# Two 33-partition copies and two stores in place of four one-row copies and one store, at the end of a decode layer

## The chip, the cores and the metric

The kernel runs on one core of a Trainium2 chip. The metric is the device time of one execution in microseconds, as the median of several runs; the span in the profile (first to last instruction) is 1.25 to 1.4 us shorter than the time of the same run. Before the change the time was 202.92 us (three runs, 202.83 to 203.02).

## The reference

One token goes through an attention block over cached keys and values (32 heads of 128, 4096 positions), then through a gated feed-forward block, both with a layer norm ahead and a residual added:

```python
h  = x + attention(layernorm(x), k_cache, v_cache, wq) @ wo     # x is [1, 1, 640], bf16
g, u = layernorm(h) @ w_gate, layernorm(h) @ w_up               # 640 -> 1728
h2 = h + (gelu(g) * u) @ w_down                                 # 1728 -> 640: the result
```

The result is 640 numbers, 1280 B.

## The kernel before

The kernel keeps lists of operations per engine. `V`, `A`, `T` add one to VectorE, ScalarE and TensorE, with the operations that it depends on; `P.dma` adds a DMA issued by the named engine. Dependencies on another engine become waits on its semaphore, a counter that the other engine raises when it is done. In these traces an issue carries one such wait itself, and one that needs two has a wait instruction ahead of it: in that of before the store's issue waits for VectorE's semaphore, and a wait instruction of 17 ns ahead of it for ScalarE's.

The last product accumulates in PSUM (`psum` in the traces, which have it as the output of these matmuls), in one tile, `ps_d`, as four rows of 160 columns in partitions 0, 32, 64 and 96. From there it is copied to `out_row` in SBUF, from which the store reads it. The residual `h` is put into the same rows first:

```python
    out_row = sb("out_row", [1, D], BF16)
    ...
    def resid(e):
        for q in range(4):
            i = e.matmul(ps_d[32 * q:32 * q + 1, 0:160], ones_f[:, 0:1],
                         hX[:, 32 * q:32 * q + 32, :].rearrange("p a c -> p (a c)"), start=True, stop=False)
        return i
    ...
    def down(ms, qs=range(4)):
        def fn(e):
            for m in ms:
                for q in qs:
                    rows, wd = (128, wd_sb[:, m]) if m < 13 else (48, wd_lo[:, m - 13])
                    i = e.matmul(ps_d[32 * q:32 * q + 1, 0:160], hm[0:rows, m:m + 1],
                                 wd[0:rows, 160 * q:160 * q + 160], start=False, stop=(m == 12))
            return i
        return fn
    ...
    T(down(range(8, 12)), d_wd[2])
    dn = {q: T(down([12], [q]), d_wd[3]) for q in (0, 2, 1, 3)}
    os = [V(lambda e, q=q: e.tensor_copy(out_row[0:1, 160 * q:160 * q + 160], ps_d[32 * q:32 * q + 1, 0:160]), dn[q])
          for q in range(2)]
    os += [A(lambda e, q=q: e.copy(out_row[0:1, 160 * q:160 * q + 160], ps_d[32 * q:32 * q + 1, 0:160]), dn[q])
           for q in range(2, 4)]
    d_out = P.dma("sync", out[0, :, :], out_row[:, :], *os)
    P.op("sync", None, d_out)          # SyncE waits for the store to land: the end of the program
```

The softmax here doesn't subtract the row's maximum and nothing guards it: scores larger than these inputs give would overflow.

## Time and profile before

| | before |
|---|---|
| time, median | 202.92 us |
| span of the profiled run | 201.52 us |
| DMA engines | busy to nine tenths or more until the last fortieth of the span |
| landing of the last piece of w_down (160 KB) to the end | 2.41 us |
| landing of the piece before it (640 KB) to the end | 2.79 us |

The change concerns what comes after the last weights. The prediction below shows the lines of the page, the chain and the timeline for it.

For comparisons I use a **tail**: the time from the start of the last four matmuls of w_down to the end of the span. It leaves out the stream of loads, whose scatter is larger than the change (the four start at 199.17 and 199.39 us in the two traces of the changed kernel below). In the timeline of before, cut to a moment at which only those four run:

```profile
199.27 0.35 PE L525 MATMUL psum<-k_slot,hm 128*1 128x160 bf16 x4
```

The four start at 199.27 us, so the tail of before is 201.52 - 199.27 = 2.26 us (2.258 from the trace's records, which are in ns).

### The profile page before, as it was taken

Reading aid. Unit: us, or ns where it says so; the run is one execution under the profiler, and the core shown is the slowest. Engines: PE = TensorE matmul, PEld = TensorE weight load, DVE = VectorE, ACT = ScalarE, POOL = GpSimd, SP = SyncE. Lnnn points to the kernel's source line nnn. Section 1 sums busy time; section 2 is a strip of 40 time slices with the busy share of each in tenths; the row PEclk is TensorE's granted clock in tenths of the full one; section 3 lists DMA queues with packets and bytes.
Section 4 is the critical chain, followed back from the end, with each engine's and each line's share of the span. In section 5 each row is a group of like instructions: output and inputs, shape, how many; then the busy total and the mean of one; then the engine's idle time right before and its main releaser. Section 6 shows DMA issues by size and latency. Waiting matters only on the chain.

```text
span 201.5 us, 2014 instructions
## 1 busy us (share of the span) xinstructions
PE 122.1 (61%) x1008; PEld 34.7 (17%) x756; DVE 100.9 (50%) x51; ACT 12.6 (6%) x33; POOL 34.4 (17%) x36
## 2 busy tenths in 40 slices
PE   0108019759908953692469439907780789479685
PEld 0101000002200120102010201100120022169583
DVE  0200196885199169608950796199229901420321
ACT  2100000001000100010001001000100010010101
POOL 6400000000063008002600170053007200100000
PEclk9999999966985995899559957975998569855555
DMA  9999999999999999999999999999999999999992
GB/s 358 415 411 455 423 429 416 429 442 455 420 429 423 423 423 475 429 416 429 423 429 423 475 423 416 429 423 429 449 449 423 423 429 408 439 420 425 411 408 80
DMA packets 3849, 84.31 MB, mean 418 GB/s; under 512 B 450, under 2 KB 644, under 8 KB 1156
## 3 DMA queue, kind: packets, MB, share of 16 engines
q1 hardware_dynamic: 3842, 84.23, 97.7%
q8 instruction: 4, 0.07, 0.1%
q14 instruction: 1, 0.01, 0.0%
q10 hardware_dynamic: 2, 0.00, 0.0%
HBM read 84.23 MB, written 0.00 MB: 418 GB/s over the span
## 4 chain that ended last, share of the span: by engine, by line
DMA 68%; PE 19%; DVE 9%; SPq 3%; issue 1%; DVEq 0%
DMA v_slot<-in_A_v_cache_dram 42%; DMA k_slot<-in_B_w_down_dram 14%; DMA k_slot<-in_A_k_cache_dram 12%; PE psum L363 9%; PE psum L167 8%; DVE prod L375 6%; SPq L59 3%; DVE sc L381 2%; PE psum L352 1%; PE psum L525 0%; DVE out_row L534 0%; DVEq L114 0%
## 5 line engine op out<-in xcount | busy, mean ns | idle before, releaser
L375 DVE TENSOR_TENSOR prod<-k_slot,qb 128x8192 bf16<-128x8192 bf16 x16 | 75.2, 4737 | 6.8 <-DMA k_slot<-in_A_k_cache_dram 4.7
L167 PE MATMUL psum<-prod,id_b 128*128 128x512 bf16 x233 | 67.1, 445 | 0.0
L381 DVE TENSOR_REDUCE sc<-psum 128x128 f32<-128x2048 f32 x8 | 18.3, 2291 | 51.0 <-PE psum L167 51.0
L385 POOL TENSOR_TENSOR p_bd<-pt,own 128x512 bf16<-128x512 bf16 x6 | 28.3, 4715 | 85.3 <-ACT pt L382 85.3
L352 PE MATMUL psum<-prod,id_b 128*128 128x512 bf16 x23 | 10.6, 461 | 49.2 <-DVE prod L375 45.7
L363 PE MATMUL psum<-v_slot,p_bd 128*16 128x512 bf16 x224 | 17.8, 475 | 7.0 <-DMA v_slot<-in_A_v_cache_dram 7.0
L352 PEld LDWEIGHTS psum<-prod,id_b 128*128 128x128 bf16 x23 | 2.3, 99 | 70.3 <-DVE prod L375 47.6
L369 PEld LDWEIGHTS psum<-hs,po_sb 128*128 128x128 f32 x64 | 9.1, 208 | 23.9 <-issue 23.5
L363 PEld LDWEIGHTS psum<-v_slot,p_bd 128*16 128x16 bf16 x224 | 5.8, 105 | 39.7 <-DMA v_slot<-in_A_v_cache_dram 28.0
L392 ACT COPY po_sb<-psum 128x512 f32<-128x512 f32 x7 | 4.1, 586 | 73.6 <-PE psum L363 73.6
L369 PE MATMUL psum<-hs,po_sb 128*128 128x4 f32 x64 | 8.5, 256 | 0.1
L335 PE MATMUL psum<-arena,xlnB 128*32 128x512 bf16 x20 | 3.3, 626 | 7.2 <-DMA arena<-in_A_wq_dram 7.2
L382 ACT ACTIVATE pt<-sc,zero_t 128x128 bf16<-128x128 f32 x8 | 3.2, 401 | 71.1 <-DVE sc L381 71.1
L465 PE MATMUL psum<-aP,arena 128*128 128x1 bf16 x160 | 6.6, 178 | 0.0
L465 PEld LDWEIGHTS psum<-aP,arena 128*128 128x128 bf16 x160 | 6.5, 131 | 0.0
L389 POOL MEMSET spare<- 1x1 f32 x1 | 0.1, 89 | 36.4 <-DVE p_bd L385 36.4
L494 PE MATMUL psum<-hlnT,v_slot 128*128 128x1 bf16 x150 | 5.5, 173 | 0.8 <-issue 0.8
L340 DVE CAST qb<-psum 128x512 bf16<-128x512 f32 x1 | 0.7, 692 | 10.1 <-PE psum L167 10.1
L494 PEld LDWEIGHTS psum<-hlnT,v_slot 128*128 128x128 bf16 x150 | 5.3, 120 | 1.5 <-issue 0.9
L363 PE MATMUL psum<-k_slot,p_bd 128*16 128x512 bf16 x32 | 2.9, 520 | 2.8 <-DVE p_bd L385 2.8
L308 PE MATMUL psum<-one_bf,x_row 1*128 1x1 bf16 x5 | 0.4, 177 | 6.8 <-DMA x_row<-in_A_x_dram 6.8
L311 DVE COPY xx<-psum 128x5 f32<-128x5 f32 x1 | 0.2, 165 | 7.2 <-PE psum L308 7.2
(72 smaller groups left out, 34.8 us busy)
## 6 DMA issues: line engine op xcount, KB each, us to landing
k_slot<-in_A_k_cache_dram SPq DMA_DIRECT2D x8, 4096.0 KB, 25.9
v_slot<-in_A_v_cache_dram SPq DMA_DIRECT2D x7, 4096.0 KB, 17.2
arena<-in_A_wq_dram SPq DMA_DIRECT2D x1, 5120.0 KB, 15.2
arena<-in_A_wo_dram SPq DMA_DIRECT2D x2, 2560.0 KB, 35.2
k_slot<-in_A_v_cache_dram SPq DMA_DIRECT2D x1, 4096.0 KB, 26.8
v_slot<-in_B_w_gate_dram SPq DMA_DIRECT2D x1, 2160.0 KB, 23.7
k_slot<-in_B_w_down_dram SPq DMA_DIRECT2D x3, 640.0 KB, 29.2
v_slot<-in_B_w_up_dram SPq DMA_DIRECT2D x1, 1296.0 KB, 26.5
```

Source lines behind the costliest of these rows:

```text
L59: ev = self.op(eng, lambda e: e.dma_start(out, in_), *deps, dma=True, chan=chan)
L167: built = e.matmul(out, lhsT, rhs, start=start, stop=stop)
L335: mm = held if hf else lambda e, *a, **k: e.matmul(*a, **k)
L352: mm = held if n or not first else lambda e, *a, **k: e.matmul(*a, **k)
L363: i = e.matmul(ps_o[a:a + 16, :], p_bd[:, 4 * b:4 * b + 4, :].rearrange("p g j -> p (g j)"), vt[:, 4 * b:4 * b + 4, :], start=(b < 4), sto ...
L369: i = e.matmul(ps_a[:, bass.ds(at, 4)], po_sb[:, 128 * r:128 * r + 128], hs[:, r, :], start=(r == 0), stop=(r == 3))
L375: mults[G, i] = VM(lambda e: e.tensor_tensor(out=prod[:, i, :, :], in0=kt[:, 64 * i:64 * i + 64, :], in1=qb[:, G, :].unsqueeze(1).to_broad ...
L381: reds[G] = VR(lambda e: e.reduce_sum(sc[:, :], ps_f.rearrange("p (g d) -> p g d", d=16), axis=AX.X), folds[G, 1])
L385: blocks[G] = on(lambda e: e.tensor_tensor(out=p_bd[:, :, :], in0=pt[:, :].unsqueeze(2).to_broadcast([128, 128, 4]), in1=own[:, :].unsquee ...
L392: evs[G] = AS(lambda e: e.copy(po_sb[:, :], ps_o), pvs[G])
L465: r = e.matmul(ps_p[:, c:c + 1], wo_sb[:, i, c::5], aP[:, i:i + 1], start=False, stop=(i == 31), skip_group_check=True)
L494: i = e.matmul(ps[:, m:m + 1], ws, hlnT[:, c:c + 1], start=(c == 0 and m == 0), stop=(c == 4), skip_group_check=True)
```

## The change

The intent is to pay for one copy per engine instead of two. A copy of 33 partitions covers two of the four rows (partitions 0 and 32, or 64 and 96) and 31 rows of no interest. The result then lies in two SBUF rows, partitions 0 and 32, of 320 columns each. Each is stored by a DMA of its own, one issued by SyncE and one by ScalarE. So that a row holds adjacent columns of the result, the product's column blocks are dealt out in the order 0, 320, 160, 480.

```diff
-    out_row = sb("out_row", [1, D], BF16)
+    out_row = sb("out_row", [33, 320], BF16)
...
+    col = (0, 320, 160, 480)
     def resid(e):
         for q in range(4):
             i = e.matmul(ps_d[32 * q:32 * q + 1, 0:160], ones_f[:, 0:1],
-                         hX[:, 32 * q:32 * q + 32, :].rearrange("p a c -> p (a c)"), start=True, stop=False)
+                         hX[:, col[q] // 5:col[q] // 5 + 32, :].rearrange("p a c -> p (a c)"), start=True, stop=False)
...
-                                 wd[0:rows, 160 * q:160 * q + 160], start=False, stop=(m == 12))
+                                 wd[0:rows, col[q]:col[q] + 160], start=False, stop=(m == 12))
...
-    dn = {q: T(down([12], [q]), d_wd[3]) for q in (0, 2, 1, 3)}
-    os = [V(lambda e, q=q: e.tensor_copy(out_row[0:1, 160 * q:160 * q + 160], ps_d[32 * q:32 * q + 1, 0:160]), dn[q])
-          for q in range(2)]
-    os += [A(lambda e, q=q: e.copy(out_row[0:1, 160 * q:160 * q + 160], ps_d[32 * q:32 * q + 1, 0:160]), dn[q])
-           for q in range(2, 4)]
-    d_out = P.dma("sync", out[0, :, :], out_row[:, :], *os)
-    P.op("sync", None, d_out)
+    dn = [T(down([12], [q]), d_wd[3]) for q in range(4)]
+    os = [V(lambda e: e.tensor_copy(out_row[0:33, 0:160], ps_d[0:33, 0:160]), dn[1]),
+          A(lambda e: e.copy(out_row[0:33, 160:320], ps_d[64:97, 0:160]), dn[3])]
+    halves = out[0, :, :].rearrange("o (q n) -> (o q) n", q=2)
+    d_out = [P.dma(eng, halves[q:q + 1, :], out_row[32 * q:32 * q + 1, :], *os) for q, eng in enumerate(("sync", "scalar"))]
+    P.op("sync", None, *d_out)
```

## The prediction

Sum: -0.30 us for the copies, 0.20 for two issues at once, 0.02 at the end, -0.08 in all, so 202.84 us. The 0.20 is the estimate from the trace of before: the 225 ns by which ScalarE's issue at the head (497 ns) is longer than the lone issue of the store (272 ns). As its mark the prediction named a second issue of about 0.45 to 0.5 us. The prediction's lines from 1.28 us on are the issues at the head (start us, us). That the wait of one issue for another is what lengthens the issue at the head was not shown.

> **What bounds the kernel now.** I read the page of the profile first, then the chain of waits cut to the last 17 us, then the order of instructions in the last 3 us, then the durations of the instructions that touch the output row, and last the waits of SyncE. The page:
>
> ```profile
> span 201.5 us, 2014 instructions
> DMA  9999999999999999999999999999999999999992
> DMA 68%; PE 19%; DVE 9%; SPq 3%; issue 1%; DVEq 0%
> DMA v_slot<-in_A_v_cache_dram 42%; DMA k_slot<-in_B_w_down_dram 14%; DMA k_slot<-in_A_k_cache_dram 12%; PE psum L363 9%; PE psum L167 8%; DVE prod L375 6%; SPq L59 3%; DVE sc L381 2%; PE psum L352 1%; PE psum L525 0%; DVE out_row L534 0%; DVEq L114 0%
> ```
>
> The DMA engines are at nine tenths or more in 39 of 40 slices of 5.04 us: the kernel streams the caches and weights, and only the last slice is not bound by them. The chain gives the copies out of PSUM (DVE out_row) 0% of the span. The change touches nothing before the last weights but the order of residual columns, so all it can win lies in the last 2.8 us. The chain of waits there (start us, us, what):
>
> ```profile
> 198.74 0.04 issue
> 198.78 0.87 PE psum L525 x20
> 199.65 0.30 DVE out_row L534
> 199.95 0.03 issue
> 199.99 0.32 DVE out_row L534
> ```
>
> After the last piece of w_down has landed come 20 matmuls (0.87 us), then two VectorE copies in a row, 0.30 + 0.03 + 0.32 = 0.65 us. The timeline of the last microseconds (start us, us, engine, line, operation) has the same, with ScalarE beside it:
>
> ```profile
> 199.64 0.66 DVE L534 CAST out_row<-psum 1x160 bf16<-1x160 f32 x2 [2.64 <-PE psum L525]
> 199.68 0.60 ACT L536 CAST out_row<-psum 1x160 bf16<-1x160 f32 x2 [5.55 <-PE psum L525]
> 200.36 0.27 SPq L59 DMA_DIRECT2D out_dram<-out_row  x1
> ```
>
> ScalarE's pair ends at 200.28, VectorE's at 200.30, and SyncE begins to issue the store at 200.36, 0.06 us after the later. From there to the end of the span is 201.52 - 200.36 = 1.16 us (201.52 is the unrounded span), of which 0.27 us is the issue and the rest the store itself. Single durations (ns min/median/max), from the view of the output row, and SyncE's wait for the landing:
>
> ```profile
> L534 DVE CAST out_row<-psum x2: 311/314/316, 199.6 to 200.0; 1x160 bf16<-1x160 f32 x2
> L536 ACT CAST out_row<-psum x2: 285/286/287, 199.7 to 200.0; 1x160 bf16<-1x160 f32 x2
> SPq L114 <- DMA out_dram<-out_row: 0.9, 1, 0.9
> ```
>
> So the tail is a series: matmuls, copy, copy, issue, flight of the store.
>
> [...]the 128-partition casts of 512 columns took 692 ns (VectorE) and 586 ns (ScalarE), and a 128-partition copy of 5 columns 165 ns. A line through those two VectorE points has (692 - 165) / 507 = 1.04 ns a column and gives 165 + 155 x 1.04 = 326 ns for 160 columns of 128 partitions; one partition took 314. So 33 partitions should cost what one does.
> [...]
>
> ```profile
> 1.28 0.33 SPq L59 DMA_DIRECT2D k_slot<-in_A_k_cache_dram  x1
> 1.30 0.50 ACTq L59 DMA_DIRECT2D x_row<-in_A_x_dram  x1
> 1.66 0.71 SPq L59 DMA_DIRECT2D v_slot<-in_A_v_cache_dram  x1
> ```
>
> ScalarE's load of one 1280 B row, issued 0.03 us into a SyncE issue, took 497 ns; SyncE's own store of one 1280 B row, with nobody beside it, took 272. SyncE's next issue, begun while ScalarE's still ran, took 707 ns, where the same load later takes 327 to 328 ns.
> [...]No part of the trace before shows two stores at once.
> [...]
>
> **The change part by part.** Copies: two per engine become one of 33 partitions by 160 columns. On VectorE the gap between its two starts goes, 199.99 - 199.64 = 0.35 us, on ScalarE 199.99 - 199.68 = 0.31 us.
>
> Start of the copies: the four last matmuls start within 0.02 us of each other[...] (the 16 matmuls before take about 0.13 us a group of four: 20 in 0.87 us). Before, VectorE waited for the first of the four and ScalarE for the second; now VectorE waits for the second and ScalarE for the fourth. I charge 0.01 us to each: VectorE starts at 199.65, ScalarE at 199.69. With 0.314 and 0.286 us they end at 199.96 and 199.98. The later end was 200.30, so both rows are ready 0.32 us earlier. I take 0.30, as the ends of matmuls are modelled.
>
> The store: SyncE waits for the same two semaphores as before, so its issue starts at about 199.98 + 0.06 = 200.04. ScalarE's issue needs the end of its own copy and VectorE's, and starts at about the same time. Both are one row of 640 B instead of 1280. Halving the bytes is worth nothing much: the store occupies a DMA engine for part of one 0.03 us slice in a flight of 0.9 us[...].
>
> Two issues at once[...]. The head gives the size: ScalarE's issue was 497 - 272 = 225 ns longer than a lone one-row issue. [...]so I estimate 0.15 to 0.27 us and take 0.20 us for the second of the two. The last store then leaves 0.20 us after the first. SyncE waits for both, so it adds to the end in full.
>
> End: one more wait on SyncE. If ScalarE's store is last it has already passed the first wait; if its own is last, a satisfied wait follows, at most 0.06 us (from the step between VectorE's end and the issue above). I take 0.02.
>
> Sum: -0.30 + 0.20 + 0.02 = -0.08 us. The span goes from 201.52 to 201.44, the time from 202.92 to about 202.84.
>
> **The rivals.** *Rival A, the two issues do not wait for each other.* Then all of the 0.30 us stays and the time is 202.62. For it: [...]the head shows three issues in a crowd of other loads[...]. Against: the 497 ns, on a one-row transfer.
>
> *Rival B, the second queue costs more than it saves.* ScalarE's queue has lain idle since its one load at 1.3 us, its sequencer must see the end of its own copy before it can issue[...]. If ScalarE's issue takes the 0.50 us of the head, and starts 0.03 us late, the time is 202.92 - 0.30 + (0.50 - 0.27) + 0.03 + 0.02 = 202.90; if the flight also lengthens by 0.1 us, 203.00. For it: the 497 and 707 ns. Against: the tail has no other DMA in flight, since the traffic ended with w_down at 198.74.
>
> *Rival C, the copies get slower with 33 partitions.* [...]Against: the 128-partition rows above.
>
> *Rival D, a change upstream.* The residual matmuls only read other columns of the same tile, same shapes and count; all loads, their order and their waits stay. I expect nothing here but the scatter of the run times (202.83 to 203.02, 0.19 us), which is more than twice the change I predict.
>
> **Range and chances.** The mechanisms span 202.62 to 203.00. With 0.1 us of scatter to either side, 202.55 to 203.10 should hold it 8 times in 10. Two per cent is 4.06 us; the whole tail from the last landing to the end is 2.8 us and half of it is untouched, so faster by 2% is impossible by this route, and slower would need something that no view shows. I give within 2% a chance of 0.99.
>
> **What would show it right or wrong.** One VectorE and one ScalarE copy of 33x160, at 0.31 and 0.29 us, starting at 199.65 and 199.69 relative to the same landing of w_down; a slower copy makes rival C right. The two issues starting within 0.1 us of each other near 200.04: [...]two at about 0.27 show rival A. From the end of the later issue to the end of the span I expect 201.52 - 200.63 = 0.89 us as before; more is the longer flight of rival B. A different time of the last w_down landing would be scatter, and the tail must then be compared from that landing on. The prediction is wrong in its main step if the tail shortens by 0.25 us or more, or grows.

## The result and the profile after

| | before | after |
|---|---|---|
| time, median of the same rounds | 202.88 us (4 runs, 202.72 to 203.02) | 202.62 us (4 runs, 202.50 to 202.70) |
| span of the profiled run | 201.52 us | 201.24 us |
| tail in the profiled run | 2.258 us | 2.072 us |

The ratio is 0.9987, with a 95% interval from 0.9970 to 1.0004: by the times alone not even certain to be faster. A ratio here is the mean time of one kernel's fast runs over that of the other's of the same rounds, so it is not quite the ratio of the medians.

The tail tells more. The timeline of after, first at a moment when only the last four matmuls run, then from the copies on (start us, us, engine, line, operation):

```profile
199.17 0.34 PE L526 MATMUL psum<-k_slot,hm 128*1 128x160 bf16 x4
...
199.55 0.32 DVE L535 CAST out_row<-psum 33x160 bf16<-33x160 f32 x1 [3.29 <-PE psum L526]
199.59 0.29 ACT L536 CAST out_row<-psum 33x160 bf16<-33x160 f32 x1 [5.99 <-PE psum L526]
199.97 0.23 ACTq L59 DMA_DIRECT2D out_dram<-out_row  x1
199.97 0.27 SPq L59 DMA_DIRECT2D out_dram<-out_row  x1
```

Each engine has one copy where it had two, and the two issues start within 5 ns of each other. Their packets are on two queues, two on q1 (SyncE's store) and two on q10 (ScalarE's). The view of the output row has the durations in ns (min/median/max), and the waits of SyncE the landing:

```profile
L535 DVE CAST out_row<-psum x1: 317/317/317, 199.6 to 199.6; 33x160 bf16<-33x160 f32 x1
L536 ACT CAST out_row<-psum x1: 289/289/289, 199.6 to 199.6; 33x160 bf16<-33x160 f32 x1
L59 ACTq DMA_DIRECT2D out_dram<-out_row x1: 227/227/227, 200.0 to 200.0; - x1
L59 SPq DMA_DIRECT2D out_dram<-out_row x1: 272/272/272, 200.0 to 200.0; - x1
...
SPq L114 <- DMA out_dram<-out_row: 1.0, 1, 1.0
```

A copy of 33 partitions costs as much as one of a single partition, within 6 ns (317 ns against 311 to 316 on VectorE, 289 against 285 to 287 on ScalarE). Neither issue is longer than the lone issue of before (272 ns): the wait of one for the other, on which the prediction put 0.20 us, is not there. The wait for the landing grew from 0.9 to 1.0 us. The profile's chain ends at ScalarE's copy now, where it ended with two VectorE copies (start us, us, what):

```profile
199.57 0.02 issue
199.59 0.29 ACT out_row L536
```

The records of both traces, in us after the start of the last four matmuls, account for the tail:

| step | before | after | difference |
|---|---|---|---|
| end of the later copy | 1.035 | 0.714 | -0.321 |
| from there to the start of SyncE's issue | 0.062 | 0.090 | +0.028 |
| start of SyncE's issue to its data packet | 0.745 | 0.818 | +0.073 |
| start of the data packet to the end of the 4 B packet behind it (9 ns) | 0.060 | 0.036 | -0.024 |
| from there to the end of the span | 0.356 | 0.414 | +0.058 |
| tail | 2.258 | 2.072 | -0.186 |

The later copy was VectorE's before (1.035; ScalarE's ended at 1.008) and is ScalarE's after. What released the issue was ScalarE's copy in both: SyncE's wait instruction for it comes first, and the issue starts 0.089 us after that copy ends before and 0.090 after. Read along that path, the first two rows are one: ScalarE's copy ends 0.294 us earlier and the issue starts 0.293 us earlier.

So 0.186 of the 0.285 us between the spans is the tail; the other 0.10 us is already there when the last four matmuls start (199.27 against 199.17); the last two pieces of w_down had landed 0.10 and 0.08 us earlier (198.63 and 199.03 against 198.74 and 199.12).

### The profile page after: what moved, and what is told of

It reads as the page before. It is cut to its first block, busy times and chain, and to the rows that moved or that the text cites. A ratio compares the mean times of both kernels' runs of the same rounds, so it can differ in the third digit from the quotient of the medians.

```text
span 201.2 us, 2014 instructions
## 1 busy us (share of the span) xinstructions
PE 119.1 (59%) x1008; PEld 34.5 (17%) x756; DVE 100.6 (50%) x50; ACT 12.3 (6%) x32; POOL 30.6 (15%) x36
## 4 chain that ended last, share of the span: by engine, by line
DMA 85%; PE 9%; SPq 4%; issue 0%; ACT 0%
DMA v_slot<-in_A_v_cache_dram 72%; DMA k_slot<-in_B_w_down_dram 14%; PE psum L363 9%; SPq L59 4%; PE psum L526 0%; ACT out_row L536 0%
## 5 line engine op out<-in xcount | busy, mean ns | idle before, releaser
L167 PE MATMUL psum<-prod,id_b 128*128 128x512 bf16 x233 | 65.0, 434 | 0.0
L352 PE MATMUL psum<-prod,id_b 128*128 128x512 bf16 x23 | 10.4, 452 | 50.5 <-DVE prod L375 47.0
L385 POOL TENSOR_TENSOR p_bd<-pt,own 128x512 bf16<-128x512 bf16 x6 | 24.4, 4071 | 89.5 <-ACT pt L382 89.5
```

Of the source, the lines that this page charges most:

```text
L167: built = e.matmul(out, lhsT, rhs, start=start, stop=stop)
L352: mm = held if n or not first else lambda e, *a, **k: e.matmul(*a, **k)
L385: blocks[G] = on(lambda e: e.tensor_tensor(out=p_bd[:, :, :], in0=pt[:, :].unsqueeze(2).to_broadcast([128, 128, 4]), in1=own[:, :].unsquee ...
```

## The experiments

**Theory.** The shorter copies give 0.32 us, and two stores in flight at once give back about 0.13: the later one is held up by 0.07 us on its way and 0.06 us in its completion. The rest of the difference is scatter ahead of the tail. **Rivals:** the tail itself is scatter; the 0.06 us is only the second wait instruction; a store of half the bytes, or a store on a second queue, is a gain in itself; one issue waits for the other, as the prediction had it.

The numbers of the tail are from the traces' records, and a table at the end of this section has them side by side. Six versions (either store alone, both stores on SyncE, the 128-row load, and the two at the head) ran once, so their state is unknown; the argument rests on their tails and issues, and not on their times. Long lines of the edits are cut with "...".

### The kernel before once more

No edit but a comment.

> The kernel before once more, only a comment differs. By tail I mean the time from the start of the last four matmuls of w_down to the end of the span: 2.26 us before, 2.07 us after. My theory (most of the 0.26 us between the medians is the shorter tail, 0.19 us, the rest is scatter ahead of it) expects a tail of 2.26 within 0.03 and a time within 0.1% of the kernel before. The rival (the tail itself varies from run to run by as much as 0.2 us, and the result is scatter) expects a tail that is off by 0.1 us or more.

Measured: tail 2.259 us, 1 ns from the first trace. Every step of the tail is within 2 ns. The time was 202.75 us (median of 6; one run of 204.41), before 202.80 beside it; ratio 1.0014, interval 0.9988 to 1.0039. The tail is thus a precise measure and the time is not: the last four matmuls started at 199.27 us in the first trace and 199.18 in this one. The rival of a scattering tail falls.

### The changed kernel once more

No edit but a comment.

> The changed kernel once more, only a comment differs, beside the next kernel on the same chip. Theory: tail 2.07 us within 0.02, time 0.05 to 0.15% below the kernel before. Rival (the first result was scatter): time within 0.05% of the kernel before.

Measured: tail 2.070 us. The time was 202.71 us (5 runs) against 202.78; ratio 0.9993, interval 0.9979 to 1.0006; the medians differ by 0.03%, below the 0.05 to 0.15% expected, and within what the rival said. The last four matmuls started at 199.39 us in this trace, 0.22 later than in the first trace of the same kernel. The gain in the tail is reproduced; a gain in time of more than that is not.

### One semaphore for both stores

```diff
-    d_out = [P.dma(eng, halves[q:q + 1, :], out_row[32 * q:32 * q + 1, :], *os) for q, eng in ...]
+    d_out = [P.dma(eng, halves[q:q + 1, :], out_row[32 * q:32 * q + 1, :], *os, chan="o") for q, eng in ...]
```

> The changed kernel, with both stores counting up one semaphore, so that SyncE waits once at the end instead of twice. Theory: of the tail after the change, 0.06 us is the second wait instruction (from the last packet to the end: 0.36 us before, 0.41 after), so the tail falls from 2.07 to 2.01. Rival: the 0.06 us is the later arrival of one of the two completions, and the tail stays at 2.07.

Measured: tail 2.087 us, from the last packet to the end 0.427. The miss is clear: with a single wait the end comes no sooner. The later of two completions arrives later in itself: it comes 0.393 us after the end of that store's packets here and 0.392 in the changed kernel, against 0.322 in the kernel before. Nor was there a second wait instruction to save: the changed kernel's trace has one wait at the end that names both semaphores. It ends 0.022 us after the last completion, where a wait for one semaphore takes 0.034, and these 0.012 us are the longer end here. The time was 202.62 us against 202.80 (ratio 0.9991, 0.9978 to 1.0004), no news beside the changed kernel.

### The copies, with one store of two rows

```diff
-    d_out = [P.dma(eng, halves[q:q + 1, :], out_row[32 * q:32 * q + 1, :], *os) for q, eng in ...]
-    P.op("sync", None, *d_out)
+    d_out = P.dma("sync", halves, out_row[0:33:32, :], *os)
+    P.op("sync", None, d_out)
```

> The changed kernel's copies, but one store of the two rows (2 x 640 B) on SyncE. Theory: the copies give 0.32 us and the pair of stores gives back some 0.13 us (0.07 in the flight, 0.06 in the second wait); one store then has a tail of 2.26 - 0.32 + 0.03 = 1.97 us (the 0.03 is the wait for ScalarE's copy, no longer covered). Rival: two stores of 640 B on two queues fly faster than one of two rows, and this tail is 2.07 or longer.

Measured: tail 2.432 us, 0.46 longer than I expected and 0.17 longer than before. The copies ended at 0.718 as in the changed kernel, so the loss is all in the store. Its issue in this run's timeline:

```profile
199.98 0.57 SPq L59 DMA_DIRECT2D out_dram<-out_row  x1
```

A store of two rows took 0.573 us to issue, where one of a single row of the same 1280 B took 0.272, and its first packet started 1.211 us after the issue began, against 0.745. Those 0.466 us are the miss. The copies with one store of two rows lose 0.17 us of the tail; the time, 202.85 us against 202.80, ratio 1.0004 (0.9991 to 1.0017), does not show it. One-row stores on two queues are what makes the change a gain in the tail. What makes this issue long stays open: the 128-row load below took 0.334 us to issue, so the number of rows alone does not, and a store of two adjacent rows was not tried. It is not the rival's reason (that two small stores fly faster), as the next run shows.

### The two stores, with the copies of before

```diff
-    d_out = P.dma("sync", out[0, :, :], out_row[:, :], *os)
-    P.op("sync", None, d_out)
+    d_out = [P.dma(eng, out[0, :, 320 * q:320 * q + 320], out_row[:, 320 * q:320 * q + 320], *os)
+             for q, eng in enumerate(("sync", "scalar"))]
+    P.op("sync", None, *d_out)
```

> The kernel before with its four copies into one row, but two stores of 640 B each on SyncE and ScalarE, both waiting for all four copies. Theory: nothing of the gain is in the stores; the tail grows by about 0.10 us (0.07 + 0.06 - 0.02), to 2.36. Rival (the stores help by half the bytes each): the tail shortens below 2.26. The step of my prediction that one issue waits for the other for 0.20 us expects 2.48 and one issue of about 0.45 us.

Measured: tail 2.359 us, 0.101 longer than before, as the theory expected to the hundredth. The issues:

```profile
200.37 0.23 ACTq L59 DMA_DIRECT2D out_dram<-out_row  x1
200.38 0.27 SPq L59 DMA_DIRECT2D out_dram<-out_row  x1
```

Neither waits for the other, and the 2.48 us of my prediction's step are not seen. The pair costs time by itself. The time was 202.93 us against 202.80 (ratio 1.0008, 0.9995 to 1.0021).

### ScalarE's store alone

The changed kernel with one of its two stores left out, so half of the output is not written; the result is wrong.

```diff
-    d_out = [P.dma(eng, halves[q:q + 1, :], out_row[32 * q:32 * q + 1, :], *os) for q, eng in ...]
-    P.op("sync", None, *d_out)
+    d_out = P.dma("scalar", halves[1:2, :], out_row[32:33, :], *os)
+    P.op("sync", None, d_out)
```

> The changed kernel with ScalarE's store of 640 B alone; half of the output stays unwritten, so the result is wrong on purpose. In the changed kernel and in the two-store kernels run so far ScalarE's packet starts 0.70 us after its issue and SyncE's 0.82, and SyncE's completion is seen 0.40 us after its last packet, where a lone SyncE store of 1280 B had 0.745 and 0.34. Theory (two stores at once hold up the later of them by 0.07 us in the flight and 0.06 in the completion): alone, ScalarE's store has 0.70 and 0.34, and the tail is 0.80 + 0.70 + 0.04 + 0.36 = 1.90 us. Rival (ScalarE's queue is the faster of the two only because it asks first): alone it has 0.745.

Measured, in the timeline:

```profile
200.01 0.23 ACTq L59 DMA_DIRECT2D out_dram<-out_row  x1
```

That is an issue of 0.227 us, 0.705 us from its start to the data packet, 0.357 from the last packet to the end, tail 1.897. In the pair ScalarE's packet came after 0.704: it is not held up. ScalarE's store was 0.040 us quicker to its packet than SyncE's (0.745, the next run), and its issue 0.044 shorter.

### SyncE's store alone

```diff
-    d_out = [P.dma(eng, halves[q:q + 1, :], out_row[32 * q:32 * q + 1, :], *os) for q, eng in ...]
-    P.op("sync", None, *d_out)
+    d_out = P.dma("sync", halves[0:1, :], out_row[0:1, :], *os)
+    P.op("sync", None, d_out)
```

> The changed kernel with SyncE's store of 640 B alone; half of the output stays unwritten, wrong on purpose. Theory (interference of the pair): 0.745 us from issue to packet and 0.34 from last packet to completion, tail 0.80 + 0.745 + 0.04 + 0.36 = 1.95 us, so 0.13 less than the pair's 2.07. Rival (a store of 640 B, or of this queue after such copies, is slow in itself): 0.82 and 0.40, tail 2.07.

Measured, in the timeline:

```profile
199.99 0.27 SPq L59 DMA_DIRECT2D out_dram<-out_row  x1
```

That is an issue of 0.271 us, packet after 0.745, last packet to the end 0.357, tail 1.943. SyncE's store of 640 B alone was as quick to its packet as that of 1280 B before (0.745 us both), and only the packets are shorter, 0.036 instead of 0.060 us. Against this, the pair's tail of 2.072 has 0.129 more: 0.818 - 0.745 = 0.073 in the flight, 0.414 - 0.357 = 0.057 in the completion. Both belong to the pair and not to the halves, which is what the theory said.

### Both stores issued by SyncE

```diff
-    d_out = [... for q, eng in enumerate(("sync", "scalar"))]
+    d_out = [... for q, eng in enumerate(("sync", "sync"))]
```

> The changed kernel with both one-row stores issued by SyncE one after the other. Theory: what the second queue saves is the issue of the first store, 0.27 us and some 0.05 of sequencer time; the second store's issue starts at 0.80 + 0.32 = 1.12 us after the last matmuls start, its packet 0.745 later, and the tail is 1.12 + 0.745 + 0.04 + 0.36 = 2.26, that of the kernel before. Rival [...]: tail 2.07 to 2.15.

Measured, in the view of line 59 (ns min/median/max):

```profile
L59 SPq DMA_DIRECT2D out_dram<-out_row x2: 248/260/272, 200.1 to 200.4; - x2
```

The tail was 2.257 us, as the theory expected; the rival was that the second queue saves next to nothing. SyncE issued for 0.272 us from 0.808 and for 0.248 from 1.122; the second packet followed its issue by 0.721 us and the end its last packet by 0.378. So the second queue saves 2.257 - 2.072 = 0.185 us, and without it the change would have left the tail where it was. These two stores, issued 0.31 us apart, did not hold each other up in flight (0.721 us, against 0.745 alone).

### A load of 128 rows beside ScalarE's issue

```diff
+    halves_in = A_k_cache[0, 0, 0:128, :]
+    big = P.dma("sync", prod[:, 0, 0, :], halves_in, *os)
     d_out = [...]
-    P.op("sync", None, *d_out)
+    P.op("sync", None, *d_out, big)
```

> The changed kernel with one more load, of 128 rows of 256 B into a tile no longer used, issued by SyncE just before its store, at the moment when ScalarE issues its own. It asks whether a 128-row issue is what held ScalarE's one-row issue at the head of the kernel (0.50 us there, 0.23 beside SyncE's one-row store). Theory[...]: ScalarE's store issue grows to 0.40 us or more. Rival (the 0.50 us came from the load of the traffic or from ScalarE's start at the head): it stays at 0.23 us.

Measured, in the timeline:

```profile
199.98 0.23 ACTq L59 DMA_DIRECT2D out_dram<-out_row  x1
199.99 0.33 SPq L59 DMA_DIRECT2D prod<-in_A_k_cache_dram  x1
200.37 0.29 SPq L59 DMA_DIRECT2D out_dram<-out_row  x1
```

ScalarE's issue took 234 ns beside a 128-row issue, 7 more than alone, and its packet came after 0.712 us. The theory that the 128-row issue holds the other up expected 0.40 us or more, and falls for this size of row. (The tail, 2.460 us, is that of the added load and the store behind it.) What lengthens the issue at the head remained to be found, for which the last two runs are.

### The table load after the input row's load

```diff
-    A(lambda e: e.preload_act_table_set("natural_log_exp_and_others"))
     d_x = P.dma("scalar", x_row[:, :], A_x[0, :, :])
+    A(lambda e: e.preload_act_table_set("natural_log_exp_and_others"))
```

> The changed kernel with ScalarE's load of the input row put ahead of its table load. It asks why that issue takes 0.50 us at the head, from which my prediction drew the 0.20 us of waiting that did not come. If the table load beside it is what lengthens it, the issue takes 0.23 to 0.30 us now. If it is SyncE's 128-row issues beside it[...], it stays at 0.45 us or more.

Measured: the issue took 508 ns. The table load alone is not the cause. The tail was 2.075 us.

### No other issue at the head

```diff
-        landed[kind][g] = P.dma("sync", dst[:, 0:128 * DH], src, after, chan=...)
+        landed[kind][g] = P.dma("sync", dst[:, 0:128 * DH], src, after, d_x if (kind, g) == order[1] else None, chan=...)
```

> The changed kernel with SyncE's third and fourth load held back until the input row has landed, so that no other issue runs beside ScalarE's at the head; slower on purpose. If an issue on SyncE beside it is the cause[...], ScalarE's takes 0.23 to 0.30 us. [...]

Measured: with no issue of SyncE between 0.9 and 2.6 us, the timeline of that window has

```profile
1.27 1.28 ACT L249 ACT_TABLE_LOAD   x1 [1.27 <-PEq L555]
1.30 0.51 ACTq L59 DMA_DIRECT2D x_row<-in_A_x_dram  x1
```

The issue is as long, 507 ns, with nobody beside it. A wait for another issue alone is not the cause. What is left is that it is the first DMA of its queue, or a load, or that the first two loads, issued from 0.00 and 0.46 us on, are under way, or that the table load and the other issue each suffice, since no run took both away; none of these was tried apart. The other reading of the prediction's lines at the head, SyncE's load of v_cache, does change: its issue took 530 to 707 ns in the thirteen traces in which it begins while ScalarE's issue runs, and 435 here, where it begins at 7.35 us. That one issue holds up another at the head is thus not excluded. The tail was 2.070 us. I had called this version slower on purpose; its single run of 202.54 us does not look slower.

### One semaphore for both copies

If both copies count up one semaphore, each store needs a single wait. In this run's trace the store's own instruction (line 59) has it, where in the changed kernel SyncE's wait for ScalarE's copy stands on a wait instruction of 17 ns (line 114).

```diff
-                    count(ev, (eng, ev.chan) if ev.chan else (eng,), 1)
+                    count(ev, ev.chan if isinstance(ev.chan, tuple) else (eng, ev.chan) if ev.chan else (eng,), 1)
...
-    os = [V(lambda e: e.tensor_copy(out_row[0:33, 0:160], ps_d[0:33, 0:160]), dn[1]),
-          A(lambda e: e.copy(out_row[0:33, 160:320], ps_d[64:97, 0:160]), dn[3])]
+    os = [P.op("vector", lambda e: e.tensor_copy(out_row[0:33, 0:160], ps_d[0:33, 0:160]), dn[1], chan=("o",)),
+          P.op("scalar", lambda e: e.copy(out_row[0:33, 160:320], ps_d[64:97, 0:160]), dn[3], chan=("o",))]
```

> The changed kernel with both copies counting up one semaphore, so that each store waits once, in its own instruction, instead of a wait instruction first (0.017 us and some 0.045 until the store begins). Theory: the two issues start 0.06 us earlier, 0.74 instead of 0.80 us after the last matmuls start, and the tail falls from 2.07 to 2.01 us. Rival (the flight of the stores is bound by something that does not move with the issue): the tail stays at 2.07. In time 0.06 us is 0.03%, below what the runs can show, so the tail decides.

Measured, in the timeline:

```profile
199.44 0.32 DVE L535 CAST out_row<-psum 33x160 bf16<-33x160 f32 x1 [3.09 <-PE psum L526]
199.48 0.29 ACT L536 CAST out_row<-psum 33x160 bf16<-33x160 f32 x1 [5.91 <-PE psum L526]
199.80 0.28 SPq L59 DMA_DIRECT2D out_dram<-out_row  x1
199.80 0.23 ACTq L59 DMA_DIRECT2D out_dram<-out_row  x1
```

The issues start 0.026 and 0.030 us after the end of ScalarE's copy instead of 0.085 and 0.090. The tail is 2.023 us, 0.049 shorter than in the first trace of the changed kernel (0.047 against the second); the expected 0.06 less what the last packet to the end took more (0.427 against 0.414). SyncE now asks 4 ns ahead of ScalarE, and its packet is still the later one, after 0.817 us: who starts first does not decide it. (ScalarE's issue, the shorter, still ended 0.045 us earlier, and no run changed that.) This is the shortest tail of a correct kernel here. Its time was 202.50 us (5 runs, 202.33 to 202.60) against 202.71 for the changed kernel and 202.78 for the kernel before; the ratio to before is 0.9987 with an interval from 0.9973 to 1.0001, so in time it is at most some 0.1 to 0.2% and not shown clear of noise.

### The steps side by side

All in us, from the traces' records; the first two columns count from the start of the last four matmuls. "Issue" is the issue of the store that landed last.

| run | later copy ends | issue starts | issue start to packet | packets | last packet to end | tail |
|---|---|---|---|---|---|---|
| before | 1.035 | 1.097 | 0.745 | 0.060 | 0.356 | 2.258 |
| before again | 1.036 | 1.096 | 0.747 | 0.060 | 0.356 | 2.259 |
| changed | 0.714 | 0.804 | 0.818 | 0.036 | 0.414 | 2.072 |
| changed again | 0.713 | 0.803 | 0.813 | 0.036 | 0.418 | 2.070 |
| one semaphore for the stores | 0.717 | 0.807 | 0.817 | 0.036 | 0.427 | 2.087 |
| one store of two rows | 0.718 | 0.808 | 1.211 | 0.060 | 0.353 | 2.432 |
| two stores, old copies | 1.033 | 1.092 | 0.804 | 0.036 | 0.427 | 2.359 |
| ScalarE's store alone | 0.713 | 0.799 | 0.705 | 0.036 | 0.357 | 1.897 |
| SyncE's store alone | 0.715 | 0.805 | 0.745 | 0.036 | 0.357 | 1.943 |
| both stores on SyncE | 0.717 | 1.122 | 0.721 | 0.036 | 0.378 | 2.257 |
| one semaphore for the copies | 0.717 | 0.743 | 0.817 | 0.036 | 0.427 | 2.023 |

The traces also record when each store's semaphore changes, twice per store: a first event well ahead of the data packet, and the completion. They divide the flight further (us):

| store | issue end to first event | first event to packet | packets' end to completion |
|---|---|---|---|
| SyncE, before (alone) | 0.161 | 0.312 | 0.322 |
| SyncE, half alone | 0.162 | 0.312 | 0.323 |
| SyncE, in the pair (changed) | 0.233 | 0.313 | 0.392 |
| ScalarE, half alone | 0.168 | 0.310 | 0.323 |
| ScalarE, in the pair (changed) | 0.169 | 0.308 | 0.328 |
| both on SyncE, the second | 0.164 | 0.309 | 0.334 |

The pair's two costs are plain here, both on SyncE's store: 0.07 us between the issue's end and the first event, and 0.07 us between the packets and the completion.

## Why the prediction was right or wrong

The time, 202.62 us, lies in the predicted range of 202.55 to 203.10 and within 2%, as predicted at 0.99. The point, 202.84, was 0.22 us too high. The range held with a wrong main step in it: 202.62 is the lower edge of what the prediction's mechanisms spanned, and the value of its rival A. Its own sign of a wrong main step, a tail shorter by 0.25 us or more, did not come either (0.186), because another cost of the pair stood in for the one that was missing. By the steps:

- **Copies.** Right. 33 partitions cost what one does (317 and 289 ns), the later copy ends 0.321 us earlier where 0.32 was worked out, and the small later start on both engines came: VectorE 0.383 instead of 0.377 us after the matmuls begin, ScalarE 0.425 instead of 0.412. Rival C is out.
- **Start of the issue.** The path was wrong, the sum nearly right. The prediction, like the profile's chain, took VectorE's copy for what the issue waits for and kept 0.06 us between the two. The records have SyncE's issue 0.089 to 0.091 us after the end of ScalarE's copy in each of the twelve traces that have such an issue behind a wait instruction, that of before included, although VectorE's copy ended 0.027 us later there. Without the wait instruction the issue follows by 0.026. So the gain on the path was 0.293 us, and not 0.32; the 0.30 of the prediction met it by luck, having been rounded down for another reason, the modelled ends of the matmuls.
- **Two issues at once.** This is the step that failed. The prediction put 0.20 us of waiting on the second issue, from the 497 ns of ScalarE's issue at the head. The issues took 227 and 272 ns together and 227 and 271 alone. The long issue at the head is as long with no issue beside it (507 ns), so it does not show the wait that the prediction read from it. In place of the 0.20 us stand 0.073 us in the flight of SyncE's store, after its issue's record; whether a wait for another issue exists at the head stays open (see the last but one experiment). Some hold-up of one store by the other is thus real, at about a third of the size and not where it was looked for.
- **End.** Mis-sized. Put at 0.02 us for a satisfied wait, it was +0.058, and not for the wait: the completion of the later store comes 0.070 us later, and the wait itself ends 0.012 us sooner. Rival B allowed for it with a flight longer by 0.1 us, an assumption that no trace of before showed. From the end of SyncE's issue to the end of the span the prediction expected 0.89 us; it was 0.996, so the flight lengthened by the 0.1 us of rival B, while the issues were as short as in rival A.
- **Bytes.** Taken as nothing; the shorter packets gave 0.024 us (a data packet of 0.031 us for 640 B, of 0.054 for 1280 B).
- **The last landing.** Misread, without effect on the sum. The prediction put 20 matmuls and 2.8 us after the last landing of w_down, 198.74. That was the landing of the piece before. The last four matmuls wait for a piece that lands at 199.12, 2.41 us before the end.

The sum was -0.30 + 0.20 + 0.02 = -0.08 us. The tail measured -0.321 + 0.028 + 0.073 - 0.024 + 0.058 = -0.186. Rival A, without a wait of the issues, expected 202.62, the very median measured, but for a wrong reason in part: it left out the 0.13 us that the pair costs, and about 0.10 us of scatter ahead of the tail makes up for it in the profiled runs. Rival D named that scatter.

What stays open: which part of the path holds up the later of two stores issued together. The packets of the pair lie 0.119 us apart in the changed kernel (0.112 again, 0.106 where SyncE asked first), and the second of two stores issued 0.31 us apart was not delayed (0.721 us to its packet, against 0.745 alone). The semaphore events narrow it down: the delay of the flight, 0.07 us, is complete at the first event, 0.31 us ahead of the packet, so it does not arise at the data packet; the second delay lies after the packets. A step that serves one store at a time for about 0.1 us, an estimate from those 0.106 to 0.119 us, would fit the first, but no run shows such a step, nor what delays the completion. The gain in time itself is not shown either: no interval of the changed kernel's ratio leaves out 1.

## What to carry to other kernels

At the end of this kernel, whose DMA engines were busy to nine tenths or more in 39 of 40 slices before the change, the way out (copy, wait, issue, flight) was a series: merging two small PSUM copies that differ only in partition took 0.29 us off it, at 3 ns more for a copy. Check by the records which copy an issue waits for: the chain named VectorE's, and the issue kept a fixed 0.09 us from ScalarE's. Before splitting or merging a store, measure its issue: here two one-row stores on two queues cost 0.13 us more than one of them alone, but one two-row store took 0.47 us more to its packet than a one-row store. Where the run times scatter by more than the change is worth, measure the stretch that the change touches, from a fixed event in the trace; here it repeated within 5 ns.
